# Attention and MoE in one kernel: VectorE's, GpSimd's and SyncE's order written out instead of planned

## The chip, the cores and the metric

The kernel runs on one core of a Trainium2 chip. The metric is the device time of one execution in microseconds. Each figure is the median of several runs. The profile shows one execution, which has a time of its own.

## The reference

The first part is attention over 8 batches, 12 heads, 448 positions and 64 values a head, with an RMS norm of q and k. The heads of a batch are laid side by side to 768 values a token, and the 3584 tokens go through a two-layer network with a quick GELU.

```python
q_n, k_n = rmsnorm(q, g_q), rmsnorm(k, g_k)      # x / sqrt(mean(x*x) + 1e-6) * g
attn = softmax(q_n @ k_n.T / sqrt(64))           # per batch and head, 448 x 448
x = (attn @ v).transpose(0, 2, 1, 3).reshape(3584, 768)
h = x @ w_in                                     # 768 x 2048
out = (h * sigmoid(1.702 * h)) @ w_out           # 2048 x 768, float32 out
```

## The kernel before

The unit of the attention is a pair of heads of one batch: `NG` = 48 pairs, six (`NP`) to a batch. The 448 positions are cut in `NS` = 4 blocks of 112 (`SS`).

The preparation of a pair has three engines. `load(i)` issues the transfers of q and k into `raw` and of v into `vraw` on SyncE (seven buffers each). `stats(i)` squares q and k on GpSimd (`sq`, L139, two buffers) and sums the squares on VectorE (`ssq`, L140); for the last pair of a group of three (the first three pairs are groups of their own) eleven small instructions on VectorE follow, which make the reciprocal root (L150 to L161, called the chain here). `norm(i)` multiplies on GpSimd (`qkn`, L169, three buffers) and casts v on VectorE (`vx`, L175).

The attention of a pair: `T(i)` transposes q and k on TensorE (`t_ps`, L182); VectorE evicts them to `qT` and `kz`. `Sc(i, kc)` makes scores of a block (`sc`, L197), ScalarE takes the exponential into `att`. `PV(i, hp)` multiplies with v for one head (`o`, L210), one PSUM bank for both heads; VectorE divides and evicts it to `obs` (L215, L216). `OT(i)` transposes the result (`ot_ps`, L225), and VectorE copies it to `xt`.

The MoE of a batch starts once its six pairs are through. Stage 1 makes 16 tiles `gp` of six matmuls (L243); ScalarE takes a tanh of each into `th`, VectorE makes `g` of both and so frees the bank (L252). Stage 2 makes output tiles `op` of 16 matmuls (L269), three token tiles for an even batch and four for an odd one, in halves; ScalarE evicts them, SyncE stores them (L290). Tiles `t_ps`, `ot_ps`, `gp` and `op` share the pool `ps_w` of three PSUM buffers.

TensorE's order is that of the code. In turn i the loop issues `Sc(i, 0..3)` with `PV(i-1, ...)`, `T(i+1)` and `OT(i-1)` between them, and in each of the four gaps `fill` adds MoE matmuls for `per_gap` = 1525 ns by its own list of prices, as long as there are any for a batch that is through. `pre(i)` stands ahead of a turn in the code, with loads six pairs ahead, `stats` five and `norm` two. For the other engines this code order doesn't bind: only TensorE is in the list of hand-ordered engines, and the framework's planner orders VectorE, ScalarE, GpSimd and SyncE by its own estimate of when each instruction can run. On the chip each engine then runs its own list strictly in order and waits at each instruction for what that needs.

Of the kernel before, what the change touches and what calls it, by code (L numbers as in the profile page):

```python
# [21 lines left out]
def kernel(  # L22
# [26 lines left out]
    ctx.enter_context(tc.manual_schedule(engines={ENG.PE}))  # L49
# [68 lines left out]

    def load(i):
# [12 lines left out]
    def stats(i):  # L132
        grp = group_of[i]
        n = len(grp)
        if i == grp[0]:
            ssq_of[grp[0]] = stat_p.tile([128, 3, 2, 2, NS], FP32, tag="ssq", name="ssq")
        ssq = ssq_of[grp[0]]
        sq = sq_p.tile([128, 2, 2, NS, D], FP32, tag="sq", name="sq")
        nc.gpsimd.tensor_tensor(out=sq[:SS], in0=raw[i][:SS], in1=raw[i][:SS], op=ALU.mult)  # L139
        nc.vector.reduce_sum(out=ssq[:SS, i - grp[0]], in_=sq[:SS], axis=AX.X)  # L140
# [3 lines left out]
        m = n * 4 * NS  # L144
        x = ssq[:SS].rearrange("p a b c d -> p (a b c d)")[:, :m]
# [57 lines left out]
    def PV(i, hp):  # L203
        att, vx = att_ring[i % N_ATT], vx_ring[i % N_V]
# [3 lines left out]
        for qs in range(NS):  # L208
            for kc in range(NS):
# [4 lines left out]
        rcp = small_p.tile([128, NS], FP32, tag="rcp", name="rcp")  # L214
        nc.vector.reciprocal(out=rcp[:SS, :], in_=o[:SS, :, D])  # L215
        nc.vector.tensor_tensor(out=obs[i][:SS, :, hp, :], in0=o[:SS, :, :D],  # L216
                                in1=rcp[:SS, :].to_broadcast([SS, NS, D]), op=ALU.mult)

    def OT(i):
        b, p = i // NP, i % NP  # L220
        if p == 0:
            xT[b] = xt_p.tile([128, KI, S], BF16, tag="xt", name="xt")
        ps = ps_w.tile([128, NS, SS], BF16, tag="w", name="ot_ps")
        for qs in range(NS):
            nc.tensor.transpose(ps[:, qs, :], obs[i][:SS, qs, :, :], ident[:SS, :SS])  # L225
        nc.vector.tensor_copy(out=xT[b][:, p, :], in_=ps[:, :, :].rearrange("p n s -> p (n s)"))  # L226
# [4 lines left out]
    def moe_list():  # L231
        items = []
        for b in range(B):
            for m in range(MI):
                box = {}

                def s1(b=b, m=m, ki=0, box=box):
                    if ki == 0:
                        if m == 0 and b % 2 == 0:
# [4 lines left out]
                                     rhs=xT[b][:, ki, :], start=(ki == 0), stop=(ki == KI - 1))  # L244
                    if ki == KI - 1:
# [12 lines left out]
            for tm in (range(3) if b % 2 == 0 else range(3, 7)):  # L258
                obox = {}
                for half in range(2):  # L260
                    box = {}

                    def s2(ko, b=b, tm=tm, half=half, box=box, obox=obox):
                        if ko == 0:
# [7 lines left out]
                            start=(ko == 0), stop=(ko == MI - 1))  # L272
                        if ko == MI - 1:
# [33 lines left out]
    LOAD, STAT, NORM = 6, 5, 2  # L307
    per_gap = 36.6e3 / (NP * 4)

    def pre(i):  # L310

        if i == 0:
            for j in range(LOAD + 1):
                load(j)
            stats(0)
            norm(0)
            for ki in range(KI):
                nc.gpsimd.dma_start(
                    out=w_in_s[:, ki, :], in_=moe_w_in[ki * 128:(ki + 1) * 128, :])
            for j in range(1, STAT + 1):  # L320
                stats(j)
                if j <= NORM:
                    norm(j)
            for ko in range(0, MI, 4):
                nc.gpsimd.dma_start(
                    out=w_out_s[:, ko:ko + 4, :],
                    in_=moe_w_out[ko * 128:(ko + 4) * 128, :].rearrange(
                        "(ko p) f -> p ko f", p=128))
            return
        if i + LOAD < NG:  # L330
            load(i + LOAD)
        if i + STAT < NG:
            stats(i + STAT)
        if i + NORM < NG:
            norm(i + NORM)

    for i in range(NG + 1):
# [49 lines left out]
```

## Time and profile before

| | |
|---|---|
| median of 3 runs | 602.76 us (600.51 to 605.67) |
| the profiled execution | 606.14 us, span 604.0 us |
| mean granted TensorE clock | 0.937 |
| busy: TensorE, VectorE, ScalarE, GpSimd | 482.9, 336.6, 268.4, 197.3 us |

The span runs from the first to the last instruction; 2.1 us of the execution lie beside it. Busy times are sums over the span, and no engine is busy throughout, so a bound has to be looked for in the waits. The granted clock is the share of full speed (2.4 GHz) that TensorE was given; its lower level is half, 1.2 GHz.

### The profile page before, as it was taken

The page shows a single profiled execution, that of the slowest core. Times are in us where ns is not written, and L with a number is a line of the kernel's source. Part 1 is how long each engine was busy: PE and PEld are TensorE (multiplying, and loading weights), DVE is VectorE, ACT ScalarE, POOL GpSimd, SP SyncE. Part 2 cuts the span into 40 slices and gives each one's busy share as a digit, 9 for nine tenths or more (in the row PEclk, how much of TensorE's full clock was granted, in tenths as well). Part 3 has the DMA queues.
Part 4 walks back from the last instruction along what each step waited for, and adds up shares of the span by engine and source line. Part 5 has one row for each costly group of instructions (what it writes and reads, how often), then busy time and mean ns, then how long its engine had stood idle before and what let it go on. Part 6 is the DMA issues. An engine that isn't in the chain of part 4 may idle for free.

```text
span 604.0 us, 10291 instructions
## 1 busy us (share of the span) xinstructions
PE 482.9 (80%) x4160; PEld 299.7 (50%) x4160; DVE 336.6 (56%) x815; ACT 268.4 (44%) x377; POOL 197.3 (33%) x167
## 2 busy tenths in 40 slices
PE   0144657898588897978698888789869999999996
PEld 0023434565345564545454555356536666666553
DVE  3367998865376637645465455665548543642520
ACT  0123454553355454644454434354436655654321
POOL 3677656333233343222532224322333121100000
PEclk9996688999799998889988899798979999999999
DMA  7999733213411253113331134211340021001012
GB/s 177 229 243 238 172 91 102 69 57 88 118 46 47 75 143 100 53 48 85 99 91 47 47 99 112 80 47 47 99 118 17 1 54 53 1 1 53 27 27 78
DMA packets 42382, 50.99 MB, mean 84 GB/s; under 512 B 3680, under 2 KB 37984, under 8 KB 42336
## 3 DMA queue, kind: packets, MB, share of 16 engines
q1 hardware_dynamic: 39360, 44.05, 26.7%
q0 software_dynamic: 2976, 6.29, 5.4%
q8 instruction: 32, 0.52, 0.4%
q14 instruction: 14, 0.11, 0.1%
HBM read 45.61 MB, written 11.01 MB: 94 GB/s over the span
## 4 chain that ended last, share of the span: by engine, by line
PE 37%; DVE 22%; DMA 20%; POOL 13%; SPq 5%; issue 2%; POOLq 0%; ACT 0%
DMA raw<-in_k_dram 18%; PE gp L243 18%; PE op L269 9%; POOL sq L139 8%; DVE ssq L140 6%; POOL qkn L169 5%; PE sc L197 5%; SPq L123 4%; PE o L210 3%; DVE kz L190 2%; DVE g L252 2%; DVE obs L216 2%; DMA vraw<-in_v_dram 2%; DVE vx L175 2%; PE t_ps L182 1%
## 5 line engine op out<-in xcount | busy, mean ns | idle before, releaser
L200 ACT ACTIVATE att<-sc 112x896 bf16<-112x896 f32 x192 | 175.2, 917 | 224.6 <-PE sc L197 223.9
L243 PE MATMUL gp<-xt,w_in_s 128*128 128x448 bf16 x768 | 175.1, 377 | 26.8 <-DVE g L252 26.8
L269 PE MATMUL op<-w_out_s,g 128*128 128x384 bf16 x896 | 159.8, 326 | 0.0
L139 POOL TENSOR_TENSOR sq<-raw 112x1024 f32<-112x1024 f32 x48 | 90.8, 1894 | 178.3 <-DMA raw<-in_k_dram 159.6
L169 POOL TENSOR_TENSOR qkn<-raw,rs 112x512 bf16<-112x512 f32 x96 | 99.8, 1061 | 139.6 <-PE t_ps L182 115.3
L243 PEld LDWEIGHTS <-w_in_s 128*128 128x128 bf16 x768 | 76.7, 103 | 100.6 <-issue 47.0
L197 PE MATMUL sc<-qT,kz 128*112 128x448 bf16 x384 | 114.9, 384 | 7.9 <-DVE kz L190 7.6
L269 PEld LDWEIGHTS <-g 128*128 128x128 bf16 x896 | 85.0, 98 | 54.5
L140 DVE TENSOR_REDUCE ssq<-sq 112x16 f32<-112x1024 f32 x48 | 58.3, 1216 | 94.3 <-POOL sq L139 94.2
L252 DVE SCALAR_TENSOR_TENSOR g<-th,gp 128x448 bf16<-128x448 f32 x128 | 78.5, 615 | 51.9 <-ACT th L249 51.9
L249 ACT ACTIVATE th<-gp 128x448 f32<-128x448 f32 x128 | 69.4, 542 | 75.5 <-PE gp L243 75.4
L210 PEld LDWEIGHTS <-att 112*128 112x128 bf16 x1536 | 64.9, 101 | 27.7 <-DVE obs L216 12.4
L210 PE MATMUL o<-vx,att 112*128 112x65 bf16 x1536 | 68.6, 199 | 9.2 <-DVE obs L216 9.2
L197 PEld LDWEIGHTS <-kz 128*112 128x112 bf16 x384 | 45.0, 142 | 20.6 <-DVE kz L190 8.9
L182 PE MATMUL t_ps<-ident,qkn 112*128 112x112 bf16 x384 | 29.8, 225 | 31.0 <-POOL qkn L169 27.1
L225 PE MATMUL ot_ps<-ident,obs 112*128 112x112 bf16 x192 | 18.9, 225 | 41.4 <-DVE obs L216 41.2
L182 PEld LDWEIGHTS <-qkn 112*128 112x128 bf16 x384 | 25.9, 105 | 41.6 <-POOL qkn L169 28.4
L190 DVE TENSOR_SCALAR kz<-t_ps,gG 64x448 bf16<-64x448 bf16 x96 | 42.8, 445 | 0.8
L275 ACT ACTIVATE osb<-op 128x384 f32<-128x384 f32 x56 | 27.4, 489 | 30.4 <-PE op L269 28.6
L216 DVE TENSOR_TENSOR obs<-o,rcp 112x256 bf16<-112x256 f32 x96 | 40.2, 419 | 1.2
L225 PEld LDWEIGHTS <-obs 112*128 112x128 bf16 x192 | 13.1, 102 | 54.2 <-DVE obs L216 50.1
L226 DVE COPY xt<-ot_ps 128x448 bf16<-128x448 bf16 x48 | 18.6, 388 | 30.1 <-PE ot_ps L225 30.0
(26 smaller groups left out, 135.8 us busy)
## 6 DMA issues: line engine op xcount, KB each, us to landing
raw<-in_q_dram SPq DMA_DIRECT2D x48, 224.0 KB, 3.1
raw<-in_k_dram SPq DMA_DIRECT2D x48, 224.0 KB, 3.8
vraw<-in_v_dram SPq DMA_DIRECT2D x48, 224.0 KB, 3.6
w_in_s<-in_moe_w_in_dram POOLq DMA_DIRECT2D x6, 512.0 KB, 11.1
w_out_s<-in_moe_w_out_dram POOLq DMA_DIRECT2D x4, 768.0 KB, 15.8
out_dram<-osb SPq DMA_DIRECT2D x8, 336.0 KB, 2.8
out_dram<-osb SPq DMA_DIRECT2D x8, 288.0 KB, 2.7
out_dram<-osb SPq DMA_DIRECT2D x8, 240.0 KB, 2.8
```

The costliest lines, as they stand in the source:

```text
L139: nc.gpsimd.tensor_tensor(out=sq[:SS], in0=raw[i][:SS], in1=raw[i][:SS], op=ALU.mult)
L140: nc.vector.reduce_sum(out=ssq[:SS, i - grp[0]], in_=sq[:SS], axis=AX.X)
L169: nc.gpsimd.tensor_tensor(out=t[:SS, gi], in0=raw[i][:SS, gi].rearrange("p h n d -> p n h d"), in1=y[:SS, a, gi].rearrange("p h n -> p n h ...
L182: nc.tensor.transpose(ps[:, gi, s, :], qkn[i][:SS, gi, s, :, :], ident[:SS, :SS])
L190: nc.vector.tensor_scalar(out=kz[r, hp, :], in0=kps[r], scalar1=gG[r, :], scalar2=None, op0=ALU.mult)
L197: nc.tensor.matmul(sc[:SS, hp, :S], lhsT=kz_ring[i % N_KZ][:, hp, kc * SS:(kc + 1) * SS], rhs=qT[i][:, :], start=True, stop=True)
L200: nc.scalar.activation(out=att_ring[i % N_ATT][:SS, kc, :, :S], in_=sc[:SS, :, :S], func=ACT.Exp)
L210: nc.tensor.matmul(o[:, qs, :], lhsT=att[:SS, kc, hp, qs * SS:qs * SS + WIN], rhs=vx[:SS, hp, kc, :], start=(kc == 0), stop=(kc == NS - 1))
L243: nc.tensor.matmul(ps[:, :], lhsT=w_in_s[:, ki, m * 128:(m + 1) * 128], rhs=xT[b][:, ki, :], start=(ki == 0), stop=(ki == KI - 1))
L249: nc.scalar.activation(out=th[:, :], in_=ps[:, :], func=ACT.Tanh, scale=0.851)
L252: nc.vector.scalar_tensor_tensor(out=g_of[b // 2][:, m, lo:lo + S], in0=th[:, :], scalar=1.0, in1=ps[:, :], op0=ALU.add, op1=ALU.mult)
L269: nc.tensor.matmul(ps[:, :], lhsT=g_of[b // 2][:, ko, tm * 128:(tm + 1) * 128], rhs=w_out_s[:, ko, half * HALF:(half + 1) * HALF], start=( ...
```

## The change

All engines are now ordered by the code. To place other engines' work, the code keeps a clock `clk` in nanoseconds that runs on with each TensorE matmul (`tick`, 48, 190, 40 or 165 a matmul). An eviction is not issued where its matmul stands, but put on a list with a due time (`later`, 250 ns behind the last matmul, 1000 for `g` and for stores), and comes in the order of these times. `need` forces due work out where the code depends on it. `stats` and `norm` are cut into `square`, `reduce`, `rsqrt`, `norm` and `vcast`, and `ahead(i, s)` places them in gap s of turn i. What comes ahead of the loop stands in `start()`.

The diff, cut to its core (`PV`, `OT`, the tanh, `g` and the output tiles are put on the list in the same way as `T` and `Sc`):

```diff
-    ctx.enter_context(tc.manual_schedule(engines={ENG.PE}))
+    ctx.enter_context(tc.manual_schedule())
...
+    clk = 0.0
+    events = []
+    seq = 0
+    done = set()
+    def later(dt, f, tag=None):
+        nonlocal seq
+        seq += 1
+        heapq.heappush(events, (clk + dt, seq, f, tag))
+    def step():
+        nonlocal clk
+        t, _, f, tag = heapq.heappop(events)
+        clk = max(clk, t)
+        f()
+        done.add(tag)
+    def tick(dt):
+        nonlocal clk
+        end = clk + dt
+        while events and events[0][0] <= end:
+            step()
+        clk = end
+    def need(*tags):
+        while any(t not in done for t in tags):
+            step()
     def load(i):
         b, h0 = i // NP, 2 * (i % NP)
...
-    def stats(i):
+    sq_of = {}
+    def square(i):
+        sq = sq_p.tile([128, 2, 2, NS, D], FP32, tag="sq", name="sq")
+        nc.gpsimd.tensor_tensor(out=sq[:SS], in0=raw[i][:SS], in1=raw[i][:SS], op=ALU.mult)
+        sq_of[i] = sq
+    def reduce(i):
...
-        nc.vector.reduce_sum(out=ssq[:SS, i - grp[0]], in_=sq[:SS], axis=AX.X)
+        nc.vector.reduce_sum(out=ssq_of[grp[0]][:SS, i - grp[0]], in_=sq_of.pop(i)[:SS],
+                             axis=AX.X)
+    def rsqrt(i):
+        grp = group_of[i]
...
         qkn[i] = t
+    def vcast(i):
         nc.vector.tensor_copy(out=vx_ring[i % N_V][:SS, :, :, :D], in_=vraw[i][:SS])
...
+                tick(48)
         t = qT_p.tile([128, NS * SS], BF16, tag="qT", name="qT")
-        kz = kz_ring[i % N_KZ]
-        nc.vector.tensor_copy(out=t[:, :], in_=ps[:, 0].rearrange("p n s -> p (n s)"))
-        kps = ps[:, 1].rearrange("p n s -> p (n s)")
-        for hp in range(2):
-            r = slice(64 * hp, 64 * hp + 64)
-            nc.vector.tensor_scalar(out=kz[r, hp, :], in0=kps[r], scalar1=gG[r, :],
-                                    scalar2=None, op0=ALU.mult)
         qT[i] = t
+        def evict():
+            kz = kz_ring[i % N_KZ]
+            nc.vector.tensor_copy(out=t[:, :], in_=ps[:, 0].rearrange("p n s -> p (n s)"))
+            kps = ps[:, 1].rearrange("p n s -> p (n s)")
+            for hp in range(2):
+                r = slice(64 * hp, 64 * hp + 64)
+                nc.vector.tensor_scalar(out=kz[r, hp, :], in0=kps[r], scalar1=gG[r, :],
+                                        scalar2=None, op0=ALU.mult)
+        later(250, evict, ("T", i))
     def Sc(i, kc):
+        need(("T", i))
...
-        nc.scalar.activation(out=att_ring[i % N_ATT][:SS, kc, :, :S],
-                             in_=sc[:SS, :, :S], func=ACT.Exp)
+            tick(190)
+        later(250, lambda: nc.scalar.activation(
+            out=att_ring[i % N_ATT][:SS, kc, :, :S], in_=sc[:SS, :, :S], func=ACT.Exp), ("E", i, kc))
...
-                        nc.scalar.activation(out=th[:, :], in_=ps[:, :], func=ACT.Tanh,
-                                             scale=0.851)
                         lo = (b % 2) * S
-                        nc.vector.scalar_tensor_tensor(
+                        later(250, lambda: nc.scalar.activation(
+                            out=th[:, :], in_=ps[:, :], func=ACT.Tanh, scale=0.851))
+                        later(1000, lambda: nc.vector.scalar_tensor_tensor(
                             out=g_of[b // 2][:, m, lo:lo + S], in0=th[:, :], scalar=1.0,
-                            in1=ps[:, :], op0=ALU.add, op1=ALU.mult)
...
-                            nc.scalar.mul(osb[:, half * HALF:(half + 1) * HALF], ps[:, :], 0.5)
+                            later(250, lambda: nc.scalar.mul(
+                                osb[:, half * HALF:(half + 1) * HALF], ps[:, :], 0.5))
                             if half == 1:
-                                store(b // 2, tm, osb)
+                                later(1000, lambda: store(b // 2, tm, osb))
...
-    LOAD, STAT, NORM = 6, 5, 2
+    LOAD, SQ, RED, NORM = 7, 6, 5, 2
     per_gap = 36.6e3 / (NP * 4)
-    def pre(i):
...
+    def start():
+        for j in range(LOAD):
+            load(j)
+        square(0)
+        reduce(0)
+        rsqrt(0)
+        norm(0)
+        vcast(0)
+        for ki in range(KI):
+            nc.gpsimd.dma_start(
+                out=w_in_s[:, ki, :], in_=moe_w_in[ki * 128:(ki + 1) * 128, :])
+        for j in range(1, SQ):
+            square(j)
+            if j < RED:
+                reduce(j)
+                rsqrt(j)
+            if j < NORM:
+                norm(j)
+                vcast(j)
+        for ko in range(0, MI, 4):
+            nc.gpsimd.dma_start(
+                out=w_out_s[:, ko:ko + 4, :],
+                in_=moe_w_out[ko * 128:(ko + 4) * 128, :].rearrange(
+                    "(ko p) f -> p ko f", p=128))
+    def ahead(i, s):
+        if s == 0:
+            if i + LOAD < NG:
+                load(i + LOAD)
+            if i + SQ < NG:
+                square(i + SQ)
+        if s == 1 and i + RED < NG:
+            reduce(i + RED)
+        if s == 2 and i + RED < NG:
+            rsqrt(i + RED)
+        if s == 3 and i + NORM < NG:
             norm(i + NORM)
+            vcast(i + NORM)
+    start()
+    T(0)
+    tick(2000)
     for i in range(NG + 1):
-        pre(i)
-        if i == 0:
...
             if s == 2 and i > 0:
                 PV(i - 1, 1)
+            ahead(i, s)
             fill(per_gap)
             if s == 1 and i + 1 < NG:
                 T(i + 1)
         if i > 0:
             OT(i - 1)
-            if i % NP == 0:
-                ready = i // NP - 1
+    tick(1000)
     fill(1e12)
+    tick(1e9)
```

TensorE's and ScalarE's instructions stand in the same order as before, tile for tile. The other three differ at nearly every place; two are shown, both of VectorE.

The first is the start, ahead of the first scores. `qT` and `kz_79` are the eviction of pair 0's transposes; `ssq<-sq` are sums of squares, and the small instructions on `ssq`, `nt` and `rs` are the chain. Before:

```order
L161 TENSOR_TENSOR rs<-rs,nt 112x16
L157 TENSOR_TENSOR nt<-rs 112x16
L158 TENSOR_TENSOR nt<-nt,ssq 112x16
L159 TENSOR_SCALAR nt<-nt 112x16
L161 TENSOR_TENSOR rs<-rs,nt 112x16
L175 CAST vx_85<-vraw 112x8x64
L186 COPY qT<-t_ps 128x448
L190 TENSOR_SCALAR kz_79<-t_ps,gG 64x448 x2
L140 TENSOR_REDUCE ssq<-sq 112x16 x2
```

And now:

```order
L197 TENSOR_TENSOR nt<-rs 112x16
L198 TENSOR_TENSOR nt<-nt,ssq 112x16
L199 TENSOR_SCALAR nt<-nt 112x16
L201 TENSOR_TENSOR rs<-rs,nt 112x16
L176 TENSOR_REDUCE ssq<-sq 112x16 x2
L232 COPY qT<-t_ps 128x448
L236 TENSOR_SCALAR kz_79<-t_ps,gG 64x448 x2
L176 TENSOR_REDUCE ssq<-sq 112x16
```

Before, the eviction stood behind pair 0's sum and chain and four casts of v; now it stands behind the sums of pairs 0 to 4 and the chains of pairs 0, 1 and 2. The chain in the second piece is that of pair 2.

The second is pair 13's transposes (`kz1_80`) in the woven part. `sq_2311` before is the square of pair 22, `sq_1506` now is that of pair 17. `rcp` and `obs` empty the bank of `PV`, `xt` that of `OT`. Before:

```order
L215 RECIPROCAL rcp_1654<-o_1637 112x4
L216 TENSOR_TENSOR obs_1636<-o_1637,rcp_1654 112x4x64
L140 TENSOR_REDUCE ssq_2173<-sq_2311 112x16
L186 COPY qT_1676<-t_ps_1667 128x448
L190 TENSOR_SCALAR kz1_80<-t_ps_1667,gG_71 64x448 x2
L215 RECIPROCAL rcp_1701<-o_1684 112x4
L175 CAST vx3_85<-vraw_1181 112x8x64
L216 TENSOR_TENSOR obs_1636<-o_1684,rcp_1701 112x4x64
L226 COPY xt_1023<-ot_ps_1708 128x448
```

And now:

```order
L268 RECIPROCAL rcp_1645<-o_1618 112x4
L269 TENSOR_TENSOR obs_1617<-o_1618,rcp_1645 112x4x64
L176 TENSOR_REDUCE ssq_1388<-sq_1506 112x16
L232 COPY qT_1664<-t_ps_1654 128x448
L236 TENSOR_SCALAR kz1_80<-t_ps_1654,gG_71 64x448 x2
L190 TENSOR_SCALAR ssq_1388<-ssq_1388 112x48
L192 TENSOR_SCALAR nt_1692<-ssq_1388 112x48
L194 TENSOR_TENSOR rs_1691<-magic_74,nt_1692 112x48
L197 TENSOR_TENSOR nt_1692<-rs_1691 112x48
```

The sum ahead of these transposes now belongs to a pair five earlier, and the whole chain of pairs 15 to 17 follows the transposes' eviction in one piece, ahead of the second `rcp`. Before, chains lay among the evictions in pieces.

## Rows read from the trace of the kernel before

**Rows 1.** Waits of TensorE, 91.07 to 508.21 us: total, times, longest.

```profile
PE ot_ps L225 <- DVE obs L216: 27.3, 14, 5.5
PE gp L243 <- DVE g L252: 26.8, 13, 3.2
PE t_ps L182 <- DVE g L252: 3.8, 2, 1.9
PE o L210 <- DVE obs L216: 2.4, 2, 1.2
```

**Rows 2.** Waits of all engines over the whole run, longest first.

```profile
POOL sq L139 <- DMA raw<-in_k_dram: 159.6, 32, 10.3
...
DVE ssq L140 <- POOL sq L139: 94.2, 29, 5.9
```

**Rows 3.** Chain that ended last, 150 to 185 us: start, us, what.

```profile
163.06 3.36 PE gp L243 x9
...
166.91 1.70 PE gp L243 x9
168.61 0.41 PE t_ps L182 x8
...
169.09 2.08 POOL qkn L169 x2
...
171.55 3.34 DMA raw<-in_k_dram
...
175.05 1.90 POOL sq L139
...
176.97 1.22 DVE ssq L140
178.19 0.54 DVE g L252
...
178.77 0.73 PE gp L243 x3
```

**Rows 4.** TensorE in order of time, from 455 us: start, us, what.

```profile
470.29 0.36 PE L225 MATMUL ot_ps<-ident,obs 112*128 112x112 bf16 x4
...
508.21 0.36 PE L225 MATMUL ot_ps<-ident,obs 112*128 112x112 bf16 x4
...
528.12 0.36 PE L225 MATMUL ot_ps<-ident,obs 112*128 112x112 bf16 x4
...
578.19 20.96 PE L269 MATMUL op<-w_out_s,g 128*128 128x384 bf16 x128
```

**Rows 5.** TensorE in order of time, first 120 us.

```profile
27.01 1.86 PE L197 MATMUL sc<-qT,kz 128*112 128x448 bf16 x4 [7.59 <-DVE kz L190]
...
50.45 0.55 PE L225 MATMUL ot_ps<-ident,obs 112*128 112x112 bf16 x4 [0.93 <-DVE obs L216]
...
84.98 0.56 PE L225 MATMUL ot_ps<-ident,obs 112*128 112x112 bf16 x4 [1.89 <-DVE obs L216]
...
91.07 0.37 PE L225 MATMUL ot_ps<-ident,obs 112*128 112x112 bf16 x4 [1.34 <-DVE obs L216]
```

**Rows 6.** VectorE in order of time, first 90 us.

```profile
12.64 1.21 DVE L140 TENSOR_REDUCE ssq<-sq 112x16 f32<-112x1024 f32 x1
...
67.62 1.78 DVE L159 TENSOR_SCALAR nt<-nt 112x48 f32<-112x48 f32 x1
```

**Rows 7.** GpSimd in order of time, first 70 us.

```profile
7.10 1.89 POOL L139 TENSOR_TENSOR sq<-raw 112x1024 f32<-112x1024 f32 x1 [5.27 <-DMA raw<-in_k_dram]
8.94 1.81 POOL L318 DMA_DIRECT2D w_in_s<-in_moe_w_in_dram  x3
16.73 2.07 POOL L169 TENSOR_TENSOR qkn<-raw,rs 112x512 bf16<-112x512 f32 x2 [5.99 <-DVE rs L161]
...
65.54 3.82 POOL L139 TENSOR_TENSOR sq<-raw 112x1024 f32<-112x1024 f32 x2 [3.66 <-DVE nt L157]
```

More of the change, by code (lines that the diff above doesn't have):

```diff
@@ L1 @@
+import heapq
 from contextlib import ExitStack
@@ L130, in load @@
         raw[i], vraw[i] = t, tv
-    def stats(i):
+    sq_of = {}
[4 more added lines that the diff above has]
+    def reduce(i):
         grp = group_of[i]
-        n = len(grp)
         if i == grp[0]:
             ssq_of[grp[0]] = stat_p.tile([128, 3, 2, 2, NS], FP32, tag="ssq", name="ssq")
-        ssq = ssq_of[grp[0]]
-        sq = sq_p.tile([128, 2, 2, NS, D], FP32, tag="sq", name="sq")
-        nc.gpsimd.tensor_tensor(out=sq[:SS], in0=raw[i][:SS], in1=raw[i][:SS], op=ALU.mult)
-        nc.vector.reduce_sum(out=ssq[:SS, i - grp[0]], in_=sq[:SS], axis=AX.X)
+        nc.vector.reduce_sum(out=ssq_of[grp[0]][:SS, i - grp[0]], in_=sq_of.pop(i)[:SS],
+                             axis=AX.X)
+    def rsqrt(i):
+        grp = group_of[i]
         if i != grp[-1]:
             return
-        m = n * 4 * NS
-        x = ssq[:SS].rearrange("p a b c d -> p (a b c d)")[:, :m]
+        m = len(grp) * 4 * NS
+        x = ssq_of[grp[0]][:SS].rearrange("p a b c d -> p (a b c d)")[:, :m]
         y = stat_p.tile([128, 3, 2, 2, NS], FP32, tag="rs", name="rs")
@@ L199, in Sc @@
                              rhs=qT[i][:, :], start=True, stop=True)
-        nc.scalar.activation(out=att_ring[i % N_ATT][:SS, kc, :, :S],
-                             in_=sc[:SS, :, :S], func=ACT.Exp)
+            tick(190)
+        later(250, lambda: nc.scalar.activation(
+            out=att_ring[i % N_ATT][:SS, kc, :, :S], in_=sc[:SS, :, :S], func=ACT.Exp), ("E", i, kc))
     def PV(i, hp):
+        need(*[("E", i, kc) for kc in range(NS)])
         att, vx = att_ring[i % N_ATT], vx_ring[i % N_V]
@@ L213, in PV, with evict @@
                                  start=(kc == 0), stop=(kc == NS - 1))
[L214 to L217, printed above, removed]
+                tick(40)
+        def evict():
+            rcp = small_p.tile([128, NS], FP32, tag="rcp", name="rcp")
+            nc.vector.reciprocal(out=rcp[:SS, :], in_=o[:SS, :, D])
+            nc.vector.tensor_tensor(out=obs[i][:SS, :, hp, :], in0=o[:SS, :, :D],
+                                    in1=rcp[:SS, :].to_broadcast([SS, NS, D]), op=ALU.mult)
+        later(250, evict, ("O", i, hp))
     def OT(i):
@@ L222, in OT @@
             xT[b] = xt_p.tile([128, KI, S], BF16, tag="xt", name="xt")
+        need(("O", i, 0), ("O", i, 1))
         ps = ps_w.tile([128, NS, SS], BF16, tag="w", name="ot_ps")
@@ L225, in OT, with evict @@
             nc.tensor.transpose(ps[:, qs, :], obs[i][:SS, qs, :, :], ident[:SS, :SS])
-        nc.vector.tensor_copy(out=xT[b][:, p, :], in_=ps[:, :, :].rearrange("p n s -> p (n s)"))
+            tick(48)
+        def evict():
+            nonlocal ready
+            nc.vector.tensor_copy(out=xT[b][:, p, :],
+                                  in_=ps[:, :, :].rearrange("p n s -> p (n s)"))
+            if p == NP - 1:
+                ready = b
+        later(250, evict, ("X", b, p))
     g_of = [None] * (B // 2)
@@ L244, in s1 @@
                                      rhs=xT[b][:, ki, :], start=(ki == 0), stop=(ki == KI - 1))
+                    tick(190)
                     if ki == KI - 1:
                         th = th_p.tile([128, S], FP32, tag="th", name="th")
-                        nc.scalar.activation(out=th[:, :], in_=ps[:, :], func=ACT.Tanh,
-                                             scale=0.851)
                         lo = (b % 2) * S
-                        nc.vector.scalar_tensor_tensor(
+                        later(250, lambda: nc.scalar.activation(
+                            out=th[:, :], in_=ps[:, :], func=ACT.Tanh, scale=0.851))
+                        later(1000, lambda: nc.vector.scalar_tensor_tensor(
                             out=g_of[b // 2][:, m, lo:lo + S], in0=th[:, :], scalar=1.0,
-                            in1=ps[:, :], op0=ALU.add, op1=ALU.mult)
+                            in1=ps[:, :], op0=ALU.add, op1=ALU.mult), ("G", b, m))
                 for ki in range(KI):
@@ L263, in s2 @@
                     def s2(ko, b=b, tm=tm, half=half, box=box, obox=obox):
+                        need(("G", b, ko))
                         if ko == 0:
@@ L305, in fill @@
             ns -= t
-    LOAD, STAT, NORM = 6, 5, 2
+    LOAD, SQ, RED, NORM = 7, 6, 5, 2
     per_gap = 36.6e3 / (NP * 4)
-    def pre(i):
-        if i == 0:
[L313 to L334, printed above, removed]
+    def start():
[33 more added lines that the diff above has]
+        if s == 3 and i + NORM < NG:
             norm(i + NORM)
+            vcast(i + NORM)
+    start()
+    T(0)
+    tick(2000)
     for i in range(NG + 1):
-        pre(i)
-        if i == 0:
-            T(0)
         for s in range(NS):
```

1 line of the change is left out of this document (added).

## The prediction

> **What bounds the kernel now.** The first view to read is the list of who waited for whom, for TensorE and the stretch in which attention and MoE run woven, from the transposes of pair 5's output to those of pair 41's [rows 1]. TensorE stands still there for 27.3 + 26.8 + 3.8 + 2.4 = 60.3 us, and behind every line stands VectorE, which has to empty a PSUM bank: `obs` of the attention, `g` of the MoE. VectorE is not short of time (336.6 us busy of 604), so the next question is what holds it. In the same view over the whole run it stood idle 94.2 us ahead of `ssq`, for the square on GpSimd, and GpSimd 159.6 us ahead of that square for the load of `raw` [rows 2]. VectorE runs its queue in order; a sum of squares whose square is not there yet stops the bank evictions behind it.
>
> The chain of waits shows it as a closed loop [rows 3]: transposes of a pair on TensorE (168.61), then the norm on GpSimd that waited for their buffer (169.09), the load into the `raw` buffer that the norm frees (171.55, 3.34 us), the square (175.05), the sum (176.97), the `g` eviction behind it (178.19), and only then the MoE matmul that wanted the bank (178.77). The order says why it is so tight: the sum ahead of pair 13's transposes is that of pair 22, nine pairs ahead of need, and `raw` has seven buffers. The load can't be earlier than the norm of pair 15, which waits for the transposes of pair 12.
>
> How much is lost is read from a stretch that waits for nothing [rows 4]: from 470.29 to 528.12 six pairs with a full share of MoE work pass in 57.83 us. A batch with an even number has one output tile less, 32 matmuls of 20.96 / 128 = 0.164 us, so 52.6. From pair 5's output (91.07 [rows 5]) to pair 41's (508.21 [rows 4]) there are three batches of each kind: 3 x (57.83 + 52.6) = 331.3 at full speed, against 417.1. So **85.8 us** are lost there: 60.3 of waits, and 25.5 of matmuls at the lower clock after them. One such place: nine stage-1 matmuls took 3.36 us from 163.06 and nine others 1.70 from 166.91 [rows 3], the 1.2 GHz level against the 2.4 GHz level.
>
> **The change part by part.** TensorE's and ScalarE's rows stand in the same order before and after, tile for tile. What moves are VectorE, GpSimd and SyncE; no instruction is added or removed.
>
> Steady state. The sum ahead of pair 13's transposes is now that of pair 17. Loads are issued seven pairs ahead, squares six, sums five. Between load and sum lie two pairs of TensorE's work (57.83 / 6 = 9.6 us each), against 3.34 + 1.90 us for load and square [rows 3]. I cost the wait for the square at nothing: the 94.2 us hide in this lead. If an output store ahead on SyncE's queue delays a load, there are still some 14 us of cover. The 60.3 us of waits [rows 1] then lose their cause, and the clock loss with them.
>
> What is late next: (a) In pairs 12, 24 and 36 the MoE work of a batch has run out, and TensorE has only the attention. VectorE's way round such a pair is: eviction of the first half, the sum of squares with the eleven `rsqrt` instructions, the transposes' eviction, the second half. The sum and chain take 16.73 - 12.64 = 4.1 us [rows 6, 7]. With the other evictions and the matmuls between them I estimate 8 us, for a pair that needs 9.64 less 37 of its 40 output matmuls (6.1), or 3.6 us, when it waits for nothing. That leaves 4.5 us of waiting and some 2 us of slow clock, three times: 20 us. (b) The chain now stands in one piece, 4.1 - 1.2 = 2.9 us, ahead of evictions. Before, it lay interleaved with them. In the woven stretch it comes 12 times, 3 of them in (a); the other 9 stand where the last `g` of a batch is still out or where ScalarE empties the banks, so I take 1 us each, 9 us. (c) Seven us for small waits elsewhere in stage 1, where three PSUM banks of the pool rotate. The rest of the loss is 36 us, taken between 15 (half of each) and 60 (each chain 3 us, and some more slow clock). So 85.8 - 36 = 50 us go.
>
> Start. In `start()` VectorE gets the sums of pairs 0 to 4 with three chains ahead of the eviction of pair 0's transposes. Before, only the first chain stood ahead. Worked out from [rows 6, 7]: square 0 ends at 9.0; sum, chain: norm 0 from 13.1 to 15.2 (16.73 before, since a cast that waited for its load stood ahead). Then come six issues of `w_in` on GpSimd, 2 x 1.81, to 18.8; square 1 to 20.7; sum and chain 1 to 24.8; norm 1 to 26.9; square 2 to 28.8; sum and chain 2 to 32.9, and up to 2 us more beside squares 3 and 4, since a single chain instruction took 1.78 us until the squares beside it ended [rows 6, 7]; then sums 3 and 4, 2.4 us, to 37; the eviction. First scores at some **38 us against 27.01** [rows 5]. Nothing covers these 11 us: TensorE has no other work yet.
>
> They come back in the pairs behind. Before, pair 0's output was transposed at 50.45, and five pairs later it is 91.07: 8.1 us a pair, with sums blocking there too. The least blocked pair took 91.07 - 84.98 = 6.1 us. With a third of a chain, 1 us, I take 7 us. From the first scores to pair 0's output it was 23.4 us, since norm 1 came only after the first scores; now it is done at 27 (above), before them, and I take 15. So 38 + 15 + 5 x 7 = 88, against 91.07: **3 us less**, with bounds from 11 less (6.1 a pair and 11 to the first output) to 11 more (nothing comes back).
>
> Sum: span 604.0 - 50 - 3 = 551; with the 2.1 us that the profiled execution has beside its span, 553. That execution was 606.14, the median of the runs is 602.76: 553 x 602.76 / 606.14 = **550 us**. The tail behind 508.21 keeps its order and waits for nearly nothing.
>
> A rule speaks against the chain in one piece. VectorE's `nt` instruction of 67.62 ends with GpSimd's squares at 69.4 [rows 6, 7]. The Trainium skill, "SBUF — State Buffer", section "Who interferes with whom", says that an instruction of VectorE with two SBUF inputs or in a two-port mode and one of GpSimd take the shared port pair as an exclusive lock for the whole instruction. The trace agrees at that row; by the rule each chain could lose up to the whole square and norm that GpSimd runs beside it.
>
> **The rivals.** *The start is not made good* (12%). The pairs behind go on at 8.1 us, because casts and chains collide with GpSimd as before; MoE begins 11 us later than 91 and not 3 earlier: 550 + 14 = 564. For it: there is such a collision at 67.62 [rows 6, 7]. Against it: the sums there no longer wait.
>
> *The chain in one piece, slower than before* (4%). At s = 1 a sum frees GpSimd's square buffer, so square and norm (1.90 + 2.07 us [rows 3, 7]) start just as the chain is queued. If they win the port, a chain takes 2.9 + 4.0 = 6.9 us, of which the three banks cover some 2; with 1.7 us of slow clock, the 3.36 less 1.70 [rows 3], each costs 6.6. Twelve of them are 79 us, with the 27 of (a) and (c) 106 against the 85.8 lost now: span 604 + 20 - 3 = 621, or 620 us. It decides from some 5 us a chain, where 12 x 5 and the 27 equal what is saved. Against it: the norm of the next group needs the chain's result, so only the square can run beside it.
>
> *It doesn't do what it says* (4%): sums still wait, because SyncE's loads stand behind stores that wait for ScalarE. Then nothing of the 85.8 goes: 603. Against it: the lead of 14 us.
>
> *Better than I take it* (10%): the rest is only (a) at half, 10 us, and the start 8 us faster: 604 - 76 - 8 + 2.1 = 522, or 519 us.
>
> **How the numbers follow.** The forecast has 70%, with a range of its own of 535 to 566 from the rest of 20 to 50 us. The range of 80% reaches from 523 to 574: down to just above the better case, up over the start that isn't made good with a rest of 46. Below it I leave 8%, above 10%. Chances: faster by over 1% is the forecast, the start rival and the better case, 0.92; within 1%, which is about what a measurement of this kernel can't tell from no change, 0.04; slower 0.04.
>
> **What would show it.** In the profile after: VectorE's wait for the square should fall from 94.2 to under 15 us, all of it ahead of 60 us. First scores at 36 to 40. Pair 5's output transposed between 80 and 100. From there to pair 41's output about 367 us and not 417, with TensorE's waits at about 25, the longest in pairs 12, 24 and 36. Granted clock 0.96 or more. I would be wrong if `rsqrt` instructions beside squares stretch over 1 us each and TensorE waits behind each chain, or if the sums still wait for squares.

## The result and the profile after

The changed kernel took 544.75 us (median of 4 runs, 544.03 to 546.09), the kernel before beside it 604.21 (4 runs, 600.51 to 607.72): a ratio of 0.902, 95% interval 0.896 to 0.908. 550 was forecast, between 523 and 574. The profiled execution took 546.09 us with a span of 543.9. Times here and below are medians of all runs of a kernel; ratios leave out the few runs that took over 1.5% longer than the fastest of the same kernel.

The waits of the changed kernel come first; columns are total, times and longest. TensorE in the woven part, from pair 5's output on, the answer to [rows 1]:

```profile
PE ot_ps L281 <- DVE obs L269: 23.1, 13, 4.8
PE op L336 <- DVE g L318: 0.2, 1, 0.2
```

VectorE and GpSimd over the whole run, the answer to [rows 2]:

```profile
DVE ssq L176 <- POOL sq L169: 13.1, 3, 7.2
...
POOL sq L169 <- DVE ssq L176: 157.8, 37, 8.0
...
POOL sq L169 <- DMA raw<-in_k_dram: 13.4, 3, 5.7
```

The arrow has turned round. Before, VectorE waited for squares, and squares for loads; now the square on GpSimd waits 157.8 us for VectorE to free its buffer by a sum, which costs nothing. The 13.1 us that VectorE still waits lie in the first 60 us. The 26.8 us in which TensorE waited for `g` ahead of `gp` are gone; 0.2 ahead of one `op` are left.

What is left is seen in TensorE's order of time:

```profile
36.80 1.85 PE L245 MATMUL sc<-qT,kz 128*112 128x448 bf16 x4 [20.89 <-DVE kz L236]
...
52.13 0.55 PE L281 MATMUL ot_ps<-ident,obs 112*128 112x112 bf16 x4 [1.07 <-DVE obs L269]
...
85.95 0.56 PE L281 MATMUL ot_ps<-ident,obs 112*128 112x112 bf16 x4 [4.82 <-DVE obs L269]
...
137.85 0.36 PE L281 MATMUL ot_ps<-ident,obs 112*128 112x112 bf16 x4
...
146.02 0.56 PE L281 MATMUL ot_ps<-ident,obs 112*128 112x112 bf16 x4 [4.36 <-DVE obs L269]
...
148.01 3.55 PE L308 MATMUL gp<-xt,w_in_s 128*128 128x448 bf16 x9
...
448.12 0.37 PE L281 MATMUL ot_ps<-ident,obs 112*128 112x112 bf16 x4 [0.85 <-DVE obs L269]
```

The first scores come 9.8 us later than before, pair 5's output 5.1 us earlier (85.95 against 91.07 [rows 5]). From there to pair 41's output it is 362.2 us instead of 417.1. From 448.12 to the end of the span it is 95.8 us, as before. At 146.02 ends one of the three turns without MoE work (but for three output matmuls at its head), with the longest wait behind that of 85.95; the nine `gp` matmuls behind it take 3.55 us, where later ones take 1.86. VectorE and GpSimd at that place:

```profile
141.13 0.90 DVE L236 TENSOR_SCALAR kz<-t_ps,gG 64x448 bf16<-64x448 bf16 x2
142.06 0.86 DVE L190 TENSOR_SCALAR ssq<-ssq 112x48 f32<-112x48 f32 x1
142.96 0.19 DVE L192 TENSOR_SCALAR nt<-ssq 112x48 int32<-112x48 int32 x1
...
145.09 0.21 DVE L201 TENSOR_TENSOR rs<-rs,nt 112x48 f32<-112x48 f32 x1
145.32 0.18 DVE L268 RECIPROCAL rcp<-o 112x4 f32<-112x4 f32 x1
145.54 0.42 DVE L269 TENSOR_TENSOR obs<-o,rcp 112x256 bf16<-112x256 f32 x1
...
140.99 1.89 POOL L169 TENSOR_TENSOR sq<-raw 112x1024 f32<-112x1024 f32 x1 [5.72 <-DVE ssq L176]
```

The chain runs from 142.06 to 145.30 in one piece, and behind it stands the eviction (145.32, 145.54) for which TensorE waits. Its first instruction took 0.86 us, until the square beside it ended (142.88); the others take 0.2.

The windows below give, in order, the length, the busy time of TensorE, its weight loads, VectorE, ScalarE and GpSimd, the granted clock, the DMA share and GB/s. All other windows of 10 us between 94 and 534 us have a clock of 1.00:

```profile
144.00:154.00 10.00, 7.98 (x46) 4.47 (x47) 5.42 (x15) 2.81 (x4) 6.17 (x5) 0.66 0.56 142
...
264.00:274.00 10.00, 7.73 (x49) 4.44 (x50) 5.78 (x16) 2.92 (x5) 5.92 (x5) 0.66 0.56 150
...
384.00:394.00 10.00, 7.56 (x51) 4.52 (x52) 6.09 (x17) 3.10 (x5) 5.75 (x5) 0.66 0.60 177
```

Each stands behind a turn without MoE work, and by its mean clock gives away 10 x 0.34 = 3.4 us.

### The profile page after: what moved, and what is told of

It reads as the page before. It is cut to its first block, busy times and chain, and to the rows that moved or that the text cites. A ratio compares the mean times of both kernels' runs of the same rounds, so it can differ in the third digit from the quotient of the medians.

```text
span 543.9 us, 10301 instructions
## 1 busy us (share of the span) xinstructions
PE 464.2 (85%) x4160; PEld 294.2 (54%) x4160; DVE 335.1 (62%) x815; ACT 267.6 (49%) x377; POOL 200.7 (37%) x167
## 4 chain that ended last, share of the span: by engine, by line
PE 73%; DVE 20%; issue 3%; POOL 2%; DMA 1%; SPq 1%; ACT 0%; POOLq 0%
PE gp L308 27%; PE op L336 23%; PE sc L245 11%; PE o L260 8%; DVE kz L236 3%; PE t_ps L224 3%; DVE ssq L176 3%; PE ot_ps L281 2%; DVE obs L269 2%; DVE ssq L190 2%; DVE nt L198 2%; DVE nt L197 1%; DVE qT L232 1%; DVE rs L201 1%; DVE nt L199 1%
## 5 line engine op out<-in xcount | busy, mean ns | idle before, releaser
L308 PE MATMUL gp<-xt,w_in_s 128*128 128x448 bf16 x768 | 164.0, 362 | 0.0
L169 POOL TENSOR_TENSOR sq<-raw 112x1024 f32<-112x1024 f32 x48 | 90.9, 1896 | 173.8 <-DVE ssq L176 157.8
L209 POOL TENSOR_TENSOR qkn<-raw,rs 112x512 bf16<-112x512 f32 x96 | 103.6, 1100 | 80.7 <-DVE rs L201 49.1
L245 PE MATMUL sc<-qT,kz 128*112 128x448 bf16 x384 | 110.9, 373 | 21.1 <-DVE kz L236 20.9
L308 PEld LDWEIGHTS <-w_in_s 128*128 128x128 bf16 x768 | 74.0, 100 | 65.2 <-issue 6.6
L176 DVE TENSOR_REDUCE ssq<-sq 112x16 f32<-112x1024 f32 x48 | 57.9, 1209 | 13.2 <-POOL sq L169 13.1
L245 PEld LDWEIGHTS <-kz 128*112 128x112 bf16 x384 | 43.6, 138 | 32.8 <-DVE kz L236 22.2
L232 DVE COPY qT<-t_ps 128x448 bf16<-128x448 bf16 x48 | 18.7, 389 | 38.4 <-PE t_ps L224 36.6
L286 DVE COPY xt<-ot_ps 128x448 bf16<-128x448 bf16 x48 | 18.5, 385 | 37.7 <-PE ot_ps L281 37.7
L224 PE MATMUL t_ps<-ident,qkn 112*128 112x112 bf16 x384 | 28.6, 219 | 15.2 <-POOL qkn L209 15.2
## 6 DMA issues: line engine op xcount, KB each, us to landing
w_out_s<-in_moe_w_out_dram POOLq DMA_DIRECT2D x4, 768.0 KB, 18.5
```

What stands on the lines that cost most here:

```text
L176: nc.vector.reduce_sum(out=ssq_of[grp[0]][:SS, i - grp[0]], in_=sq_of.pop(i)[:SS], axis=AX.X)
L209: nc.gpsimd.tensor_tensor(out=t[:SS, gi], in0=raw[i][:SS, gi].rearrange("p h n d -> p n h d"), in1=y[:SS, a, gi].rearrange("p h n -> p n h ...
L245: nc.tensor.matmul(sc[:SS, hp, :S], lhsT=kz_ring[i % N_KZ][:, hp, kc * SS:(kc + 1) * SS], rhs=qT[i][:, :], start=True, stop=True)
L308: nc.tensor.matmul(ps[:, :], lhsT=w_in_s[:, ki, m * 128:(m + 1) * 128], rhs=xT[b][:, ki, :], start=(ki == 0), stop=(ki == KI - 1))
```

## The experiments

The theory: the lead decides. Sums that stand nine pairs ahead of the transposes' eviction must wait for a square that can't be made yet, and hold bank evictions; at four they don't. And what is left is the chain standing in one piece ahead of an eviction. Rivals: another engine's list brings the gain; more buffers would have done; the turns without MoE work are long whatever VectorE does. Ratios are to the kernel before, with 95% intervals; "woven part" is the time from pair 5's output to pair 41's (331.3 us without loss, 362.2 in the changed kernel, 417.1 before).

### Which engine's list

```diff
-    ctx.enter_context(tc.manual_schedule())
+    ctx.enter_context(tc.manual_schedule(engines={ENG.PE, ENG.DVE}))
```

> The changed kernel with only TensorE and VectorE ordered by the code; GpSimd, SyncE and ScalarE are left to the planner, which puts GpSimd's squares 2 to 4 pairs ahead of the norm (4 when all are ordered by the code, 6 before) and loads of v elsewhere. Theory (VectorE's sums stood nine pairs ahead of the transposes, as early as the buffers allow, and blocked the evictions behind them; at four they don't): the whole gain is VectorE's list, 540 to 552 us, waits of TensorE for evictions of stage 1 near 0. Rival (the lead of loads and squares on SyncE and GpSimd brings it): most of the gain is lost, 580 to 605 us.

It took 547.48 us, 0.909 (0.901 to 0.916), the woven part 362.2 as in the changed kernel. VectorE's order by hand carries the gain; those of ScalarE, GpSimd and SyncE add nothing that can be measured.

```diff
-    ctx.enter_context(tc.manual_schedule())
+    ctx.enter_context(tc.manual_schedule(engines={ENG.PE, ENG.Activation, ENG.Pool, ENG.SP}))
```

> The changed kernel with all engines but VectorE ordered by the code; the planner orders VectorE, and now puts its sums 5 to 7 pairs ahead of the transposes (9 before, 4 in the changed kernel), with pair 0's eviction first in the start and chains in pieces. Theory (it is the lead of the sums that counts, and 6 or 7 still leave a pair of time for load and square): as fast as the changed kernel in the woven part, and first scores some 10 us earlier: 535 to 550 us. Rival (VectorE's list written by hand is what brings it, its chain in one piece and its due times): 570 to 605 us.

570.06 us, 0.946 (0.939 to 0.954): the theory's time was missed, and the rival's range begins here. The planner put the sums 5 to 7 pairs ahead, and they still waited. The waits of VectorE, GpSimd and SyncE say how:

```profile
DVE ssq L176 <- POOL sq L169: 40.1, 21, 3.5
...
POOL sq L169 <- DMA raw<-in_k_dram: 139.0, 18, 17.2
...
SPq L359 <- ACT osb L343: 358.6, 28, 33.4
```

SyncE stood 358.6 us ahead of stores whose eviction wasn't done, and the loads of the next pairs stood behind them in its list. In the changed kernel it stands there for 277.2 us too, but the loads behind are for pairs whose sums are far off. This looks like the cause; the mechanism is tested below, in another kernel. The first scores came at 20.3 us here, and pair 0's output at 52.7, no earlier than in the changed kernel. Still, 35 of some 60 us came without VectorE's order by hand: with the other lists by hand the planner itself puts the sums less far ahead.

### How far ahead the sums stand

The changed kernel, with loads, squares, norms and sums of later pairs pulled forward step by step, until from pair 13 on the sum ahead of each eviction is that of the ninth pair behind it (with `more` at most 4, and the sum at s = 1, of the eighth):

```diff
-    stat_p = pool("stat", 3)
+    stat_p = pool("stat", 6)
...
+        more = max(0, min(5, i - 7))
         if s == 0:
-            if i + LOAD < NG:
-                load(i + LOAD)
-            if i + SQ < NG:
-                square(i + SQ)
...
+            if i >= 8:
+                upto("norm", i + 3, norm)
+            upto("v", i + LOAD, load_v)
+            upto("qk", i + max(LOAD, RED + more), load_qk)
+            upto("sq", i + max(SQ, RED + more), square)
+            if more == 5:
+                sums(i + 10)
+        if s == 1 and more < 5:
+            sums(i + RED + more)
...
```

> All engines ordered by the code as in the changed kernel, but from pair 8 on the lead grows until the sum that stands ahead of a pair's transposes is nine pairs ahead, as before the change; loads and squares are moved ahead with it, as early as the seven buffers allow. Start and tail are those of the changed kernel. Theory (a sum that stands so early waits for the loop of transposes, norm, load and square): VectorE waits 60 to 100 us for squares, TensorE's waits behind it come back, 575 to 600 us. Rival (the lead is harmless, the gain is the order of the rest, such as due times and the stores' place): 543 to 550 us.

608.03 us, 1.007 (1.002 to 1.012): the lead, with the loads, squares and norms that it takes along, takes back the whole gain, more than expected. The woven part took 416.7 us.

```profile
DVE ssq L184 <- POOL sq L177: 78.2, 27, 8.3
...
SPq L156 <- POOL qkn L217: 142.1, 25, 13.4
```

The loads stand 142.1 us behind norms that free their buffer, against 16.4 in the changed kernel. In the kernel before, this was the largest of SyncE's waits, taken together:

```profile
SPq L123 <- POOL qkn L169: 218.0, 33, 13.6
```

> The kernel in which the sum of squares stood nine pairs ahead of the transposes' eviction (it lost all of the gain), with one pair less: eight. Theory A (what decides is whether the square that a sum waits for can only be made from a buffer that is freed behind that sum's own turn; with one pair less the loop of norm, load, square and sum has a turn of slack, 9 to 10 us against the 4 us of a load, 1.9 of a square and 2.1 of a norm): VectorE's waits for squares stay under 25 us, time 541 to 550. Theory B (each pair of lead costs its share): a fifth less than the loss at nine, time 585 to 600.

576.9 us, 0.952 (0.946 to 0.958): neither theory's number. VectorE waited 50.8 us for squares and GpSimd 77.9 for loads, but SyncE only 3.1 us for norms. One place; SyncE, GpSimd and VectorE in order of time:

```profile
180.84 0.45 SPq L156 DMA_DIRECT2D raw<-in_k_dram  x1
195.59 1.15 SPq L367 DMA_DIRECT2D out_dram<-osb  x2
...
197.96 0.47 SPq L156 DMA_DIRECT2D raw<-in_k_dram  x1
...
202.10 1.89 POOL L177 TENSOR_TENSOR sq<-raw 112x1024 f32<-112x1024 f32 x1 [4.35 <-DMA raw<-in_k_dram]
...
204.03 1.22 DVE L184 TENSOR_REDUCE ssq<-sq 112x16 f32<-112x1024 f32 x1 [2.13 <-POOL sq L177]
```

The loads of 197 us come right behind two stores that were issued at 195.6, after 14 us without an issue. So the same kernel was run with the stores in another list:

```diff
-            nc.sync.dma_start(
+            nc.scalar.dma_start(
                 out=out[b * S:(b + 1) * S].rearrange("(ss ns) d -> ns ss d", ns=NS)[ns, ss:ss + n],
```

> The kernel with the sums eight pairs ahead (576.9 us), with one change: the stores of the output are issued by ScalarE behind the eviction that they store, instead of by SyncE, where the loads of the next pairs stand behind them. Theory A (at eight ahead the loop has slack, but the loads wait in SyncE's list behind stores whose eviction is not yet done, in the six pairs of each dozen that carry output matmuls; this is also what kept the planned vector list at 570): VectorE's waits for squares fall from 50.8 to under 15 us, POOL's waits for loads from 77.9 to under 30, time 541 to 553, of which a few us may be ScalarE's 56 issues of about 0.4 us each. Theory B (the loop of buffers itself is too tight at eight): waits for squares stay above 40 us, time 565 to 585.

544.22 us, 0.900 (0.896 to 0.903), the woven part 353.5 us instead of 388.2:

```profile
DVE ssq L184 <- POOL sq L177: 13.9, 5, 7.2
...
POOL sq L177 <- DMA raw<-in_k_dram: 11.3, 2, 6.1
```

At eight pairs ahead the buffers have slack, and what held the sums was the loads' place behind the stores. That 544 us comes level with the changed kernel is in part another gain: at this lead the chains fall in turns 11, 14, 17 and so on, none of them in a turn without MoE work. The kernel with shifted groups (below) has them there too, at a lead of four; it takes 533.33 us with a woven part of 349.9, which is 3.6 us less than here, and its pair 5's output comes 5.1 us earlier. So the rival "it doesn't do what it says" of the prediction is real at a lead of eight; at four it is covered. That the planned vector list lost its 25 us in the same way is likely from its waits, but it wasn't run with the stores moved; nor was the lead of nine. In the changed kernel, from pair 13 on, each square is done 14.2 to 18.7 us before its sum begins.

### More buffers in the kernel before

```diff
-    raw_p = pool("raw", 7)
+    raw_p = pool("raw", 9)
```

> The kernel before with nine raw buffers instead of seven, all else left to the planner, which now puts the sums 11 pairs ahead of the transposes and not 9. Theory (the planner moves a sum as far ahead as the buffers allow, so that the loop is as tight as before): no change within 2%, 592 to 612 us, VectorE still waits some 90 us for squares. Rival (the loads were short of buffers): half or more of the gain, 545 to 575 us.

587.07 us, 0.975 (0.966 to 0.983): faster than the 592 to 612 of the theory, and far from the rival. The planner moved the sums on from nine to eleven pairs ahead, and they waited 80.8 us in 29 places as before (94.2 in 29), each shorter (3.8 at most instead of 5.9). The two buffers more went for the most part into lead and not into slack.

### What is left: the chain in one piece

Groups cut so that no chain falls in a turn without MoE work:

```diff
-    groups = [[0], [1], [2], [3, 4, 5]] + [list(range(j, j + 3)) for j in range(6, NG, 3)]
+    groups = [[0], [1], [2], [3, 4]] + [list(range(j, min(j + 3, NG))) for j in range(5, NG, 3)]
```

> The hand-ordered kernel with the groups of the Newton step cut as 0, 1, 2, 3-4, then threes from 5: the same chains of small operations, none of them any longer in the turns in which TensorE gets no MoE work (pairs 12, 24, 36). TensorE's and ScalarE's orders stay. Theory A (those three turns of 8.2 us, with a wait of 4.4, are long because the chain stands ahead of the eviction of the transposed outputs there, and the slow clock of 6.8 us follows from the idle stretch): each comes to 4.5 to 6 us, the three clock dips go, and the time falls by 8 to 16 us, to 529 to 537; some of the other chains now cost 1 us each. Theory B (a turn without fill is long by itself, since its own chain of scores, exponential, output, eviction is): turns stay at 7 to 8.5 us, time 541 to 548.

533.33 us, 0.883 (0.879 to 0.888): theory A. The turn without MoE work takes 142.19 - 137.27 = 4.92 us instead of 8.17, and the matmuls behind it have the full clock:

```profile
137.27 0.37 PE L281 MATMUL ot_ps<-ident,obs 112*128 112x112 bf16 x4
...
142.19 0.37 PE L281 MATMUL ot_ps<-ident,obs 112*128 112x112 bf16 x4 [1.10 <-DVE obs L269]
...
143.29 1.87 PE L308 MATMUL gp<-xt,w_in_s 128*128 128x448 bf16 x9
```

Smaller portions of MoE work, so that no turn is without any:

```diff
-    per_gap = 36.6e3 / (NP * 4)
+    per_gap = 33.6e3 / (NP * 4)
```

> The hand-ordered kernel with MoE portions a gap of 33.6/24 us by its own clock instead of 36.6/24: the MoE work of one pair of batches lasts until the next is ready, so that no turn is left without any (TensorE's order changes, the amount of work doesn't). Theory A (the turns without fill and the half clock behind them cost 15 to 19 us of the 31 lost in the woven part): the waits at pairs 12, 24 and 36 go, the dips behind them too, granted clock of the woven part 0.99 or more; time 526 to 532. Theory B (VectorE's work of a turn sets the pace, TensorE only seems to): the time stays within 541 to 548, with the waits spread over all turns.

543.82 us, 0.900 (0.895 to 0.905): theory A's time fails, but its waits go in two places of three. In pairs 24 and 36 the last gap of the turn now has nine output matmuls, and the waits fell from 4.36 and 4.35 us to 0.36 and 0.37. In pair 12 the work ran out just ahead of the last gap, and TensorE still waits, behind the same chain (140.81 to 144.45 on VectorE). Pair 12, then pair 24:

```profile
141.24 0.54 PE L245 MATMUL sc<-qT,kz 128*112 128x448 bf16 x2
145.18 0.55 PE L281 MATMUL ot_ps<-ident,obs 112*128 112x112 bf16 x4 [3.39 <-DVE obs L269]
...
258.62 1.63 PE L336 MATMUL op<-w_out_s,g 128*128 128x384 bf16 x9
260.61 0.37 PE L281 MATMUL ot_ps<-ident,obs 112*128 112x112 bf16 x4 [0.36 <-DVE obs L269]
```

So these turns are long by two things together, the chain and a gap without matmuls to cover it. Filling them brought little time, since smaller portions cover less elsewhere: 1.95 us of wait at 321.1, where the changed kernel has 0.4 to 0.9, and seven waits of up to 2.4 us for a bank that `g` frees. The waits behind pair 5's output add up to 19.3 us, against 18.5 in the changed kernel, and the tail takes 100.3 us instead of 95.8.

The chain in three pieces, with groups, turns and other engines' orders as in the changed kernel:

```diff
+        pieces.extend([seed, newton, newton])
...
         if s == 2 and i + RED < NG:
             rsqrt(i + RED)
         if s == 3 and i + NORM < NG:
             norm(i + NORM)
             vcast(i + NORM)
+        if s > 0:
+            piece()
```

`rsqrt` only lists the pieces here, the first three instructions and two Newton steps of four; `piece` issues the next.

> The hand-ordered kernel with the chain of small operations cut in three (three operations ahead of the second output's eviction, four behind it, four in the next turn behind the sum); groups, turns and all other engines' orders stay, and so does the number of operations. Theory A (what TensorE waits for in every third turn is the chain's length in one piece ahead of that eviction): the wait of the turns without MoE work falls from 4.4 to 1.5 to 3 us, the other chains' waits of 0.4 to 0.9 go, one or more of the three half-clock stretches go; time 527 to 538. Theory B (those turns are long by VectorE's total work, or by waiting for GpSimd at the shared port, which three starts meet three times): 541 to 550.

523.34 us, 0.866 (0.861 to 0.870): more than theory A had. The woven part fell to 342.6 us, and the turn without MoE work to 140.13 - 133.86 = 6.27:

```profile
140.13 0.37 PE L292 MATMUL ot_ps<-ident,obs 112*128 112x112 bf16 x4 [2.45 <-DVE obs L280]
...
138.08 0.86 DVE L198 TENSOR_SCALAR ssq<-ssq 112x48 f32<-112x48 f32 x1
...
139.65 0.42 DVE L280 TENSOR_TENSOR obs<-o,rcp 112x256 bf16<-112x256 f32 x1
...
140.32 0.20 DVE L206 TENSOR_TENSOR nt<-rs 112x48 f32<-112x48 f32 x1
```

TensorE's waits behind pair 5's output are 7.4 us in three places (18.5 in 13 in the changed kernel, without the 4.8 at 85.95), and of the windows of 10 us between 94 and 514 us only one has a lower clock. The same instructions, spread, cost some 20 us less.

### The start

```diff
     def start():
...
+        square(1)
+        T(0)
+        need(("T", 0))
+        sums(1)
+        prep(1)
+        weights_in()
+        square(2)
+        square(3)
+
+    first = {
+        (0, 2): lambda: (need(("T", 1)), sums(2), prep(2), square(4)),
+        (0, 3): lambda: (sums(3), square(5)),
...
```

> The hand-ordered kernel with another order at its start alone: the transposes of pair 0 and their eviction come ahead of the sums of pairs 1 to 4 in VectorE's list, both weights are fetched later, and the squares and sums of the next pairs are placed among the first turns until they are five pairs ahead; TensorE's and ScalarE's orders stay. Theory A (the front is bound by VectorE's list: TensorE's first scores at 36.8 us wait for pair 0's eviction, which stands behind five pairs of sums): first scores 17 to 22 us, pair 5's output 66 to 78 instead of 86, time 527 to 538. Theory B (the front is bound by what the first pairs' loads and the weights let through, as the kernel with the planned vector list had its first scores at 20 and pair 0's output no earlier): first scores early, pair 5's output 82 to 90, time 541 to 549.

542.21 us, 0.898 (0.894 to 0.902). The first scores moved from 36.8 to 16.4 us, and pair 5's output only from 85.95 to 83.05: theory B. Where the 20 us went, TensorE, VectorE and GpSimd in order of time:

```profile
64.12 0.55 PE L281 MATMUL ot_ps<-ident,obs 112*128 112x112 bf16 x4 [11.17 <-DVE obs L269]
...
55.07 4.33 DVE L190 TENSOR_SCALAR ssq<-ssq 112x48 f32<-112x48 f32 x1
59.44 1.81 DVE L192 TENSOR_SCALAR nt<-ssq 112x48 int32<-112x48 int32 x1
...
55.39 2.12 POOL L209 TENSOR_TENSOR qkn<-raw,rs 112x512 bf16<-112x512 f32 x2
57.42 3.77 POOL L169 TENSOR_TENSOR sq<-raw 112x1024 f32<-112x1024 f32 x2
```

The chain's first instruction lasted 4.33 us, beside two norms and a square on GpSimd, and its second 1.81, until the last square ended (61.19). Pair 2's output stood behind the chain for 11.17 us. From 42 to 82 us VectorE was busy 34.6 of 40 us and GpSimd 31.2, and the DMA engines 0.97 of the time. Which of the three sets the pace of these pairs wasn't taken apart.

Start and smaller portions together:

> Both edits in one kernel: the mended start and the smaller portions. If front and woven part are separate terms, their gains add: by the theories A of the two, 510 to 522; by one A and one B, 526 to 538; by both B, 541 to 549. Against a sum: an earlier front brings the MoE of the first batches no earlier if the weights land late, and then less than the sum is left.

540.32 us, 0.896 (0.891 to 0.901), just under the 541 to 549 of both theories B: two small gains, about what the two gave alone.

Mended start, shifted groups and the chain in pieces:

> Three edits together: the mended start, the groups shifted so that no chain falls in a turn without MoE work, and the chain in three pieces. Where the shifted groups alone gave 533.3, the waits left there were the chains in the turns with the first MoE matmul (7 turns of 11.9 instead of 10 us) and the start. By theory A these go too, and the start gives 3 us as it did by itself: 514 to 524. By theory B (VectorE's work of those turns is too long in any order): 528 to 534.

520.87 us, 0.862 (0.857 to 0.866), the fastest, though not to be told from the chain in pieces alone (0.861 to 0.870). Pair 5's output comes at 80.97 us and the woven part takes 341.9. TensorE is now busy 463.3 of 518.7 us:

```profile
PE 463.3 (89%) x4160; PEld 295.7 (57%) x4160; DVE 325.1 (63%) x826; ACT 267.9 (52%) x377; POOL 199.0 (38%) x167
```

## Why the prediction was right

The forecast was 5 us above the time. Its mechanism held where the runs tested it. Sizes of its terms were off, not all the same way, so that in part it is luck that the sum came so near. Its own range of 535 to 566 is worked out for the span; as a time it is 534 to 564.

- **The loop of sums.** Held: 13.1 us of waits for squares, all early, where under 15 were forecast; TensorE's waits for `g` ahead of `gp` gone. The lead was shown to be the cause by putting it back, with what it takes along (608 us), and by one engine's list alone (547 us). Stores ahead of loads, against which the forecast set 14 us of cover, do cost 576.9 - 544.2 = 33 us at a lead of eight; at four no sum behind the start waits.
- **The start.** First scores 36.80 (38 forecast), pair 0's output 52.13 (53), pair 5's 85.95 (88). The reasons behind the pace of 7 us a pair weren't settled: even with the scores 20 us earlier pair 5's output moved by 3.
- **The rest of the loss**, 36 forecast, 362.2 - 331.3 = 30.9 measured, with errors that offset each other. (a) The three turns without MoE work: 8.17 us each, against 8 estimated, waits of 4.36, 4.36 and 4.35 and 3.4 us of clock behind each: 13.1 + 10.2 = 23.3 instead of 20, since the slow clock was taken at 2 us. (b) The other chains: 5.2 instead of 9, at 0.4 to 0.9 us each. (c) Small waits in stage 1: 0.2 instead of 7; this term had no row behind it. The remaining 2.2 are the slow clock that runs on from the start. The forecast's (a) has both the chain and the missing work, and the runs bear out both: of the wait of 4.36 us, 1.10 is left with the chain moved away, 2.45 with the chain cut, and in two of the three turns 0.36 with the last gap filled. Only the first two shortened the run, since filling cost as much elsewhere.
- **The chain as a rival.** It was never stretched to the 6.9 us that would have made the kernel slower: in the woven part it takes 2.5 to 3.2, and beside one square its first instruction loses 0.7 us. Nine of the twelve chains cost 0.4 to 0.9 us. The three in turns without MoE work, with 4.36 us of wait and 3.4 of clock, do cost more than the 6.6 of the rival, but by their place and not by GpSimd. The rival's mechanism is there at the start (last section).
- **The tail** was 95.8 us on both sides. The granted clock was 0.957 where 0.96 or more was forecast.

## What to carry to other kernels

An engine that runs its list in order needs each item late enough that its input is surely there, and no earlier: look at what the longest wait ahead of a cheap instruction holds up, and count its lead against the buffers that its input needs; a planner turns added buffers into more lead. Then look at the same list for a long run of small instructions that stands ahead of an eviction, and cut it into pieces where the eviction falls between them: here that gave 20 us more for no instruction less. And keep loads off a queue on which they stand behind stores that wait for results.

## What the runs showed of the hardware

One small instruction of VectorE can last through several of GpSimd's. In the changed kernel, VectorE and GpSimd at 40 us:

```profile
40.70 5.08 DVE L190 TENSOR_SCALAR ssq<-ssq 112x48 f32<-112x48 f32 x1
45.81 0.19 DVE L192 TENSOR_SCALAR nt<-ssq 112x48 int32<-112x48 int32 x1
...
39.92 1.94 POOL L169 TENSOR_TENSOR sq<-raw 112x1024 f32<-112x1024 f32 x1
41.78 2.10 POOL L209 TENSOR_TENSOR qkn<-raw,rs 112x512 bf16<-112x512 f32 x2
43.80 1.92 POOL L169 TENSOR_TENSOR sq<-raw 112x1024 f32<-112x1024 f32 x1
```

An instruction that takes 0.19 us elsewhere lasted 5.08, through four GpSimd instructions back to back, and ended with the last (45.72). The lock that the prediction cited from the Trainium skill ("SBUF — State Buffer", "Who interferes with whom") is held for one instruction; the trace agrees that VectorE then waits to its end. Whether VectorE gets its turn between two of GpSimd's that follow at once, the same trace shows both ways. Above it got none at three such places. At 29 us, beside three squares back to back, it got one:

```profile
29.52 0.59 DVE L190 TENSOR_SCALAR ssq<-ssq 112x16 f32<-112x16 f32 x1
30.14 1.82 DVE L192 TENSOR_SCALAR nt<-ssq 112x16 int32<-112x16 int32 x1
...
26.34 5.59 POOL L169 TENSOR_TENSOR sq<-raw 112x1024 f32<-112x1024 f32 x3
```

The first instruction ended at 30.11, while the squares went on, and the second lasted to the end of the last square (31.93). What decides between the two isn't known. Sums and evictions from PSUM beside GpSimd kept their time (sums 1.21 to 1.22 us with and without it). That this is the lock and not something else that ends with GpSimd's instructions wasn't tried by itself.
